# Idle matmuls ahead of the first loads, and attention loads moved from SyncE's queue to GpSimd's

## The chip, the cores and the metric

The kernel runs on one core of a Trainium2 chip. The metric is the device time of one execution in microseconds (us); the time of a kernel is the median of its runs. Engines are named as in the profile: PE is TensorE's matmul, PEld its weight load, DVE VectorE, ACT ScalarE, POOL GpSimd, SP SyncE, which issues most transfers.

## What is computed

Causal attention with a local mask (heads 0 to 3: the last 32 positions) and a strided mask (heads 4 to 7: same position modulo 32), then two MLPs one behind the other, all in float32. Weights arrive as 64-bit floats and are converted on the chip.

```
q, k, v: (4, 8, 576, 64)          # batch, heads, positions, head size
scores = q @ k.T / sqrt(64), masked with local (h < 4) or strided (h >= 4)
x  = softmax(scores) @ v          # transposed to (2304, 512)
h  = relu(x @ w_in)               # w_in (512, 2048)
x2 = (s * h*h + b) @ w_out        # w_out (2048, 512)
out = ((x2 @ w_a) * (x2 @ w_b)) @ w_o2
```

## The kernel before

The 2304 tokens are worked in six blocks of 384 columns. Block 0 holds positions 0 to 95 of the four batches, block 1 positions 96 to 191, and blocks 2 to 5 the rest of one batch each. The attention of block n+1 is worked in steps between the matmuls of block n's first MLP; block 0's attention has nothing to run beside and goes first.

**The first stage** (lines 758 to 782). `first_mask` builds the mask `fmask` on GpSimd: half 0 is local (L315, L319), half 1 strided (three selects, L324). `first_load` loads q, k and v of 96 positions for each batch on SyncE, 192 KB each; `stage_next` loads a pair of weight pieces (512 KB of `w_in` and 512 KB of `w_out`). Then `first` runs for each batch bb: PE transposes q and k (`fps`, L116), ACT copies them out (`fqkT`, L347), PE multiplies (`fss`, L113), the softmax follows (L210 on DVE adds the mask and takes the maximum, L216 on ACT is the exponential, L221 to L223 on DVE normalise), PE transposes the result (`fpp`), ACT copies it (`fpT`, L366), PE multiplies with v (`fpo`), and ACT and DVE split the product into a high and a low part of `x` (L131, L132). The tile `fqkT` of batch 0 lies in the one buffer with the tag "sk", which the second block's strided attention loads into afterwards.

**Weight conversion** (`to_float32`): L153 on ACT, L157, L160 and L163 on DVE, then the split L131 and L132. It is worked in the first stage too, in the gaps.

**Block 0's first MLP** then starts with `h_mm`: 12 matmuls of 128x384, the first that need all of `x`.

**Block 1's attention** (`local` with n == 1, and `strided_one`) is loaded ahead on SyncE: qn, kn, vn for the local heads and sk, sv for the strided ones.

A scheduler that models the engines' times (`schedule_with_timeline_sim=True`) sets the order of the instructions on each engine; on the chip each engine then takes them strictly in that order. A DMA issue waits at the head of its engine's queue until its buffer is free and until the DMA eight issues back in the same kind of queue has landed, since each kind has eight semaphores in turn (DMAHW0 to 7 for SyncE, DMASW0 to 7 for GpSimd in the order rows below).

Of the kernel before, what the change touches and what calls it, by code (L numbers as in the profile page):

```python
# [8 lines left out]
F32 = mybir.dt.float32  # L9
# [8 lines left out]
P = 128  # L18
# [8 lines left out]
def sparse_attention_two_mlps(  # L27
# [22 lines left out]
    nc = tc.nc  # L50
    B, H, S, D = q.shape
# [60 lines left out]
    def mm(*args, **kwargs):  # L112
        last_pe[:] = [nc.tensor.matmul(*args, **kwargs).ins]  # L113
# [118 lines left out]
    def local(spans, n, hp_, c0):  # L232


        (ba, ta), (bz, tz) = spans
        joint = ba == bz
        wk = QT if joint else P
        nk = (wk + P) // 2
# [5 lines left out]
        else:  # L244
            pieces = [(ba, ta, QT, 0, 0), (bz, tz, QT, QT // 2, P // 2)]
        for bb, t0, m, pq, pk in pieces:
            nc.sync.dma_start(
                out=qn[pq:pq + m // 2],
                in_=q[bb, hs, t0:t0 + m, :].rearrange("h (p j) d -> p h (j d)", j=2),
            )  # L250
            nc.sync.dma_start(
                out=kn[pk:pk + (m + STR) // 2],
                in_=k[bb, hs, t0 - STR:t0 + m, :].rearrange("h (p j) d -> p h (j d)", j=2),
            )
# [15 lines left out]
                    )  # L270
        yield
        for j, (bb, t0) in enumerate(spans):
            nc.sync.dma_start(
                out=vn[:, j], in_=v[bb, hs, t0 - STR:t0 + QT, :].rearrange("h t d -> t h d")
            )
        yield
# [33 lines left out]
    def first_mask():  # L310

        m = slot(wpa, [QT, 2, QT], "fmask")
        nc.gpsimd.memset(m[:, 0], 0.0)
        nc.gpsimd.memset(m[:, 1], NEG)
        nc.gpsimd.affine_select(  # L315
            out=m[:, 0], in_=m[:, 0], compare_op=ALU.is_ge, fill=NEG, base=0,
            pattern=[[-1, QT]], channel_multiplier=1,
        )
        nc.gpsimd.affine_select(  # L319
            out=m[:, 0], in_=m[:, 0], compare_op=ALU.is_gt, fill=NEG, base=STR,  # L320
            pattern=[[1, QT]], channel_multiplier=-1,
        )
        for i in range(IQ):
            nc.gpsimd.affine_select(  # L324
                out=m[:, 1], in_=m[:, 1], compare_op=ALU.not_equal, fill=0.0, base=-i * STR,
                pattern=[[-1, QT]], channel_multiplier=1,
            )
        return m

    def first_load(dst, src, bb):  # L330
        nc.sync.dma_start(out=dst, in_=src[bb, :, 0:QT, :].rearrange("h t d -> t h d"))
# [151 lines left out]
    def strided_one(pair, i):  # L483
# [6 lines left out]
        for j in range(2):  # L490
            bb = 2 * i + j
            for h in range(2):
                head = HL + 2 * pair + h
                nc.sync.dma_start(
                    out=sk[:QT, 3 * j:3 * j + 2, h], in_=k[bb, head, 0:TU].rearrange("(c p) d -> p c d", p=QT)
                )
                nc.sync.dma_start(out=sk[:QT, 3 * j + 2, h], in_=q[bb, head, QT:TU])
        yield
        kqT = tl([P, S], "skT")
        for j in range(2):  # L500
# [4 lines left out]
        yield  # L505
        for j in range(2):
            for h in range(2):
                nc.sync.dma_start(
                    out=sv[:QT, 2 * j:2 * j + 2, h],
                    in_=v[2 * i + j, HL + 2 * pair + h, 0:TU].rearrange("(c p) d -> p c d", p=QT),  # L510
                )
# [228 lines left out]
    def column_sums():  # L740
# [16 lines left out]
        nc.vector.tensor_copy(out=b_col, in_=pc)  # L757
        yield

    fmask = first_mask()  # L760
    qks, vs = [], []
    for bb in range(B):
# [4 lines left out]
    for bb in range(B):  # L767
        first_load(qks[bb][:, 0], q, bb)
        first_load(qks[bb][:, 1], k, bb)
        if bb % 2:  # L770
            first_load(vs[bb - 1], v, bb - 1)
            first_load(vs[bb], v, bb)
            stage_next()
    banks = ((ps_acc, "acc"), (ps_a, "a"), (ps_acc, "acc"), (ps_a, "a"))
    gens = [first(bb, qks[bb], vs[bb], fmask, *banks[bb]) for bb in range(B)]
    live, step = list(range(B)), 0
# [97 lines left out]
```

## Time and profile before

| | |
|---|---|
| median of 3 runs | 1040.44 us (1040.05 to 1041.5) |
| the profiled execution | 1042.37 us |
| its span | 1040.5 us |
| PE busy | 997.3 us (96%) |
| DVE busy | 470.0 us (45%) |
| ACT busy | 461.7 us (44%) |
| POOL busy | 72.6 us (7%) |

The span runs from the first to the last instruction of the profiled execution. A busy share is a mean over the whole span; the stages differ, so the first 150 us are read from windows of their own. The granted TensorE clock is 1.00 at the upper of two levels (2.4 GHz) and 0.50 at the lower (1.2 GHz).

### The profile page before, as it was taken

How to read it: one execution, taken by the hardware profiler on the slowest of the kernel's cores; microseconds unless marked ns; L12 is line 12 of the kernel's file. 1: busy time of each engine (PE TensorE's matmuls, PEld its weight loads, DVE VectorE, ACT ScalarE, POOL GpSimd, SP SyncE). 2: the span in 40 equal slices, each digit the busy share in tenths (PEclk: the TensorE clock that was granted, in tenths of full speed). 3: DMA queues.
4: the chain of work that ended last, by engine and by line, in shares of the span. 5: the costliest groups of instructions: out<-in, count | busy, mean ns of one | idle time of the engine just before them, and what ended most of it. 6: DMA issues, size and time to landing. Idle time of an engine off the chain costs nothing.

```text
span 1040.5 us, 15811 instructions
## 1 busy us (share of the span) xinstructions
PE 997.3 (96%) x5984; PEld 936.0 (90%) x5984; DVE 470.0 (45%) x1246; ACT 461.7 (44%) x1291; POOL 72.6 (7%) x110
## 2 busy tenths in 40 slices
PE   6878979999999899999999999999999999999998
PEld 5768979999899899889999989999999999999997
DVE  5689755766878677576522221211211211211111
ACT  6677846665675666567532231311311311211212
POOL 3000000001233132100000000000000000000000
PEclk9988989999999999999999999999999999999999
DMA  9556422456454554644567710200200100000000
GB/s 190 190 185 183 152 56 78 144 157 195 142 142 136 175 138 139 194 140 148 192 196 252 249 32 2 61 1 1 61 1 1 61 1 1 31 1 1 31 1 30
DMA packets 109819, 106.37 MB, mean 102 GB/s; under 512 B 59568, under 2 KB 94640, under 8 KB 109744
## 3 DMA queue, kind: packets, MB, share of 16 engines
q1 hardware_dynamic: 104560, 86.49, 28.9%
q0 software_dynamic: 5184, 18.88, 4.8%
q8 instruction: 47, 0.77, 0.3%
q14 instruction: 28, 0.23, 0.1%
HBM read 77.03 MB, written 28.31 MB: 101 GB/s over the span
## 4 chain that ended last, share of the span: by engine, by line
PE 85%; DVE 6%; ACT 5%; DMA 3%; issue 1%; SPq 0%; ACTq 0%; DVEq 0%
PE acc L113 30%; PE h L113 18%; PE pb L113 14%; PE pa L113 14%; PE pss L113 2%; PE po L113 2%; PE ppt L116 2%; DMA o<-o1s 1%; DMA xr<-o 1%; PE fss L113 1%; DVE raw L160 1%; DVE w L132 1%; DVE raw L163 1%; DVE raw L157 1%; ACT r L560 1%
## 5 line engine op out<-in xcount | busy, mean ns | idle before, releaser
L113 PE MATMUL h<-x,w 128*128 128x384 f32 x1152 | 229.2, 348 | 3.4 <-DVE w L132 1.3
L113 PE MATMUL acc<-gt,w 128*128 128x384 f32 x1152 | 223.0, 341 | 3.2 <-ACT o1s L586 3.2
L113 PEld LDWEIGHTS h<-x,w 128*128 128x128 f32 x1152 | 205.4, 194 | 7.9 <-DVE w L132 1.6
L113 PEld LDWEIGHTS acc<-gt,w 128*128 128x128 f32 x1152 | 199.4, 189 | 7.4 <-ACT o1s L586 3.8
L641 DVE TENSOR_TENSOR ab<-pb,ab 128x384 f32<-128x384 f32 x72 | 40.1, 557 | 306.7 <-ACT ab L640 306.7
L113 PE MATMUL pb<-x,w 128*128 128x384 f32 x864 | 165.0, 337 | 0.0
L113 PE MATMUL pa<-x,w 128*128 128x384 f32 x864 | 162.1, 335 | 1.5 <-ACT ab L640 1.5
L113 PE MATMUL acc<-w,abt 128*128 128x512 f32 x648 | 161.8, 393 | 0.0
L640 ACT ACTIVATE ab<-pa 128x384 f32<-128x384 f32 x72 | 35.4, 491 | 282.4 <-PE pa L113 282.3
L113 PEld LDWEIGHTS pb<-x,w 128*128 128x128 f32 x864 | 153.6, 188 | 6.4 <-DVE x L132 0.3
L113 PEld LDWEIGHTS pa<-x,w 128*128 128x128 f32 x864 | 150.8, 188 | 2.6 <-ACT ab L640 2.5
L113 PEld LDWEIGHTS acc<-w,abt 128*128 128x128 f32 x648 | 120.5, 188 | 21.9
L560 ACT ACTIVATE r<-h 128x384 f32<-128x384 f32 x96 | 46.8, 488 | 115.6 <-PE h L113 115.3
L567 DVE TENSOR_TENSOR r<-r 128x384 f32<-128x384 f32 x80 | 48.8, 610 | 91.1 <-ACT gt L566 90.5
L132 DVE TENSOR_TENSOR abt<-ab,abt 128x384 fp32r<-128x384 f32 x72 | 40.2, 558 | 46.8 <-ACT abt L131 46.8
L131 ACT ACTIVATE w<-raw 128x512 fp32r<-128x512 f32 x68 | 44.8, 670 | 25.7 <-DVE raw L163 21.6
L568 DVE TENSOR_TENSOR gt<-r,gt 128x384 fp32r<-128x384 f32 x80 | 54.1, 676 | 4.5
L132 DVE TENSOR_TENSOR w<-raw,w 128x512 fp32r<-128x512 f32 x68 | 45.9, 685 | 21.7 <-ACT w L131 20.8
L131 ACT ACTIVATE abt<-ab 128x384 fp32r<-128x384 f32 x72 | 37.7, 524 | 40.2 <-DVE ab L641 40.2
L604 POOL DMA_DIRECT2D w2d<-w x36 | 20.0, 556 | 431.6 <-DVE w L132 358.9
L163 DVE SCALAR_TENSOR_TENSOR raw<-raw 128x512 uint32<-128x512 uint32 x68 | 46.5, 686 | 0.7
L160 DVE SCALAR_TENSOR_TENSOR raw<-raw 128x512 uint32<-128x512 uint32 x68 | 45.9, 685 | 0.5
(109 smaller groups left out, 878.7 us busy)
## 6 DMA issues: line engine op xcount, KB each, us to landing
w2d<-w POOLq DMA_DIRECT2D x36, 512.0 KB, 5.2
w<-w2d SPq DMA_DIRECT2D x36, 512.0 KB
raw<-in_moe_w_out_dram SPq DMA_DIRECT2D x28, 512.0 KB
raw<-in_moe_w_in_dram SPq DMA_DIRECT2D x16, 512.0 KB
raw<-in_moe_w_a_dram SPq DMA_DIRECT2D x12, 512.0 KB
raw<-in_moe_w_b_dram SPq DMA_DIRECT2D x12, 512.0 KB
xr<-o SPq DMA_DIRECT2D x6, 768.0 KB
o<-o1s SPq DMA_DIRECT2D x20, 192.0 KB
```

The lines of the kernel that those rows point to most:

```text
L113: last_pe[:] = [nc.tensor.matmul(*args, **kwargs).ins]
L116: last_pe[:] = [nc.tensor.transpose(*args).ins]
L131: nc.scalar.activation(out=hi, in_=src, func=AF.Copy)
L132: return eng_lo.tensor_tensor(out=lo, in0=src, in1=hi.bitcast(F32), op=ALU.subtract)
L160: nc.vector.scalar_tensor_tensor(out=low, in0=high, scalar=3, in1=low, op0=ALU.logical_shift_left, op1=ALU.bitwise_or)
L163: nc.vector.scalar_tensor_tensor(out=high, in0=high, scalar=0x80000000, in1=low, op0=ALU.bitwise_and, op1=ALU.bitwise_or)
L560: relu = nc.scalar.activation(out=r, in_=ph, func=AF.Relu)
L567: nc.vector.tensor_tensor(out=r, in0=r, in1=r, op=ALU.mult)
L568: lo = nc.vector.tensor_tensor(out=gt[:, 1], in0=r, in1=gt[:, 0].bitcast(F32), op=ALU.subtract)
L604: stores.append(nc.gpsimd.dma_start(out=w2d[i - 1], in_=w.bitcast(F32)).ins)
L640: nc.scalar.activation(out=ab, in_=pa, func=AF.Copy)
L641: nc.vector.tensor_tensor(out=ab, in0=pb, in1=ab, op=ALU.mult)
```

## The change

Three edits. Ahead of the first stage PE gets 14 matmuls of the identity with itself into a PSUM tile that nobody reads. The loads of block 1's attention, in `local` and in `strided_one`, are issued by GpSimd in place of SyncE. The four v loads of the first stage go behind the first two pairs of weight pieces.

```diff
@@ local
         (ba, ta), (bz, tz) = spans
+
+        queue = nc.gpsimd if n == 1 else nc.sync
         joint = ba == bz
@@
         for bb, t0, m, pq, pk in pieces:
-            nc.sync.dma_start(
+            queue.dma_start(
                 out=qn[pq:pq + m // 2],
...
-            nc.sync.dma_start(
+            queue.dma_start(
                 out=kn[pk:pk + (m + STR) // 2],
...
         for j, (bb, t0) in enumerate(spans):
-            nc.sync.dma_start(
+            queue.dma_start(
                 out=vn[:, j], in_=v[bb, hs, t0 - STR:t0 + QT, :].rearrange("h t d -> t h d")
             )
@@ strided_one
-                nc.sync.dma_start(
+                nc.gpsimd.dma_start(
                     out=sk[:QT, 3 * j:3 * j + 2, h], in_=k[bb, head, 0:TU].rearrange("(c p) d -> p c d", p=QT)
                 )
-                nc.sync.dma_start(out=sk[:QT, 3 * j + 2, h], in_=q[bb, head, QT:TU])
+                nc.gpsimd.dma_start(out=sk[:QT, 3 * j + 2, h], in_=q[bb, head, QT:TU])
@@
-                nc.sync.dma_start(
+                nc.gpsimd.dma_start(
                     out=sv[:QT, 2 * j:2 * j + 2, h],
@@ the first stage
+    idle = ps_acc.tile([P, P], F32, tag="acc", name="idle")
+    for _ in range(14):
+        mm(idle, lhsT=ident, rhs=ident, start=True, stop=True)
+
     fmask = first_mask()
@@
         first_load(qks[bb][:, 0], q, bb)
         first_load(qks[bb][:, 1], k, bb)
         if bb % 2:
-            first_load(vs[bb - 1], v, bb - 1)
-            first_load(vs[bb], v, bb)
             stage_next()
+    for bb in range(B):
+        first_load(vs[bb], v, bb)
```

The lines below `local` move down by 2, those below the idle matmuls by 7. The scheduler makes a new order from the new program. Three places of it:

GpSimd's queue in the first stage, before (the selects of `fmask`, with those of the later masks `smask` and `omask` between them):

```order
L315 AFFINE_SELECT fmask_178<-fmask_178 96x96 [waits Pool_49]
L324 AFFINE_SELECT fmask_178<-fmask_178 96x96 [waits Pool_49]
L193 AFFINE_SELECT smask_148<-smask_148 84x126 [waits Pool_49]
L193 AFFINE_SELECT omask_149<-omask_149 96x192 [waits Pool_49]
L319 AFFINE_SELECT fmask_178<-fmask_178 96x96 [waits Pool_49]
```

and the same place of the change (sv and sk are block 1's strided loads; ten loads of qn, kn, vn and sv are issued by then):

```order
L326 AFFINE_SELECT fmask_193<-fmask_193 96x96 [waits Pool_49]
L510 DMA sv_614<-in_v_dram 96x2x64 [waits DMASW0_49]
L510 DMA sv_614<-in_v_dram 96x2x64 [waits DMASW1_49]
L496 DMA sk_613<-in_k_dram 96x2x64 [waits DMASW2_49,PE_49,Activation_49]
L321 AFFINE_SELECT fmask_193<-fmask_193 96x96 [waits Pool_49]
L499 DMA sk_613<-in_q_dram 96x64 [waits DMASW3_49]
L496 DMA sk_613<-in_k_dram 96x2x64 [waits DMASW4_49]
L499 DMA sk_613<-in_q_dram 96x64 [waits DMASW5_49]
L496 DMA sk_613<-in_k_dram 96x2x64 [waits DMASW6_49]
L326 AFFINE_SELECT fmask_193<-fmask_193 96x96 [waits Pool_49]
```

The last select of `fmask`'s local half (L321) now stands behind the first sk load, which waits for PE, and the last two of its strided half (L326) behind all eight sk loads.

DVE at the start, before (the first softmax, then the first weight piece):

```order
L210 ISA fpt_229,mx_240<-fss_230,fmask_178 96x96 [waits PE_49,Pool_49]
L210 ISA fpt_229,mx_250<-fss_235,fmask_178 96x96 [waits PE_49]
L221 TENSOR_SCALAR sm_241<-sm_241 96x4 [waits Activation_49]
L222 RECIPROCAL sm_241<-sm_241 96x4 [waits DVE_49]
L157 TENSOR_SCALAR raw_202<-raw_202 128x512 [waits DMAHW0_49]
```

and of the change, from the first softmax on (raw_223 is the second piece of w_in, raw_225 the second of w_out; the first two pieces are worked ahead of this):

```order
L210 ISA fpt_244,mx_265<-fss_250,fmask_193 96x96 [waits PE_49]
L157 TENSOR_SCALAR raw_223<-raw_223 128x512 [waits DMAHW4_49]
L160 SCALAR_TENSOR_TENSOR raw_223<-raw_223 128x512 [waits DVE_49,Activation_49]
L157 TENSOR_SCALAR raw_225<-raw_225 128x512 [waits DMAHW5_49]
L163 SCALAR_TENSOR_TENSOR raw_223<-raw_223 128x512 [waits DVE_49]
L160 SCALAR_TENSOR_TENSOR raw_225<-raw_225 128x512 [waits DVE_49,Activation_49]
L163 SCALAR_TENSOR_TENSOR raw_225<-raw_225 128x512 [waits DVE_49]
L210 ISA fpt_244,mx_255<-fss_245,fmask_193 96x96 [waits Pool_49]
```

Four of the 32 L210 (batch 0's local heads) now stand ahead of the second pair of weight pieces and 28 behind it, and the pair waits for its loads (DMAHW4 and DMAHW5).

SyncE's queue, before:

```order
L331 DMA fv<-in_v_dram 96x8x64 x2
L139 DMA raw<-in_moe_w_in_dram 128x4x256
L144 DMA raw<-in_moe_w_out_dram 128x1024
L247 DMA qn<-in_q_dram 48x2x128
L251 DMA kn<-in_k_dram 64x2x128
```

and of the change:

```order
L333 DMA fqk<-in_k_dram 96x8x64
L139 DMA raw<-in_moe_w_in_dram 128x4x256
L144 DMA raw<-in_moe_w_out_dram 128x1024
L333 DMA fv<-in_v_dram 96x8x64 x4
L406 DMA sq<-in_q_dram 128x3x64 x2
```

Before, twelve loads of 96x8x64 and four weight pieces stand up to the end of the second pair; in the change eight and four, with the v loads behind.

## Rows read from the trace of the kernel before

**Rows 1.** Windows: busy us (count) of PE, PEld, DVE, ACT, POOL; granted clock, DMA share, GB/s.
```profile
10.98:39.39 28.41, 25.18 (x166) 20.59 (x165) 23.82 (x109) 24.68 (x92) 0.08 (x1) 1.00 0.96 241
60.00:140.00 80.00, 67.07 (x448) 62.94 (x446) 70.81 (x185) 63.15 (x171) 0.00 (x0) 0.91 0.48 148
...
600.00:700.00 100.00, 99.08 (x520) 92.24 (x519) 21.51 (x40) 26.67 (x55) 0.00 (x0) 1.00 0.09 25
```

**Rows 2.** Timeline, first stage: start, duration, engine, line, what, idle before and releaser.
```profile
5.01 0.26 POOL L324 TENSOR_SCALAR_AFFINE_SELECT fmask<-fmask 96x96 f32<-96x96 f32 x1
...
10.69 0.26 DVE L210 CUSTOM_DVE_ANT_0 fpt<-fss,fmask 96x96 f32<-96x96 f32 x1 [9.34 <-PE fss L113]
...
14.50 0.43 DVE L157 TENSOR_SCALAR raw<-raw 128x512 uint32<-128x512 uint32 x1 [0.41 <-DMA raw<-in_moe_w_out_dram]
...
24.38 0.42 DVE L157 TENSOR_SCALAR raw<-raw 128x512 uint32<-128x512 uint32 x1
...
38.90 0.49 ACT L131 ACTIVATE x<-fpo 128x384 fp32r<-128x384 f32 x1 [0.48 <-PE fpo L113]
...
40.81 3.89 PE L113 MATMUL h<-x,w 128*128 128x384 f32 x11 [0.68 <-DVE x L132]
```

**Rows 3.** Groups of ACT by form, 10.9 to 39.4 us: count, busy us, mean ns, idle before.
```profile
L216 ACT ACTIVATE fpt<-fpt,mx 96x96 f32<-96x96 f32 x32 | 11.6, 364 | 3.8 <-DVE mx L210 3.8
...
L366 ACT ACTIVATE fpT<-fpp 96x384 f32<-96x384 f32 x8 | 3.8, 481 | 1.9 <-PE fpp L116 1.9
L153 ACT ACTIVATE raw<-raw 128x512 f32<-128x512 f32 x6 | 3.8, 671 | 0.0
...
L131 ACT ACTIVATE w<-raw 128x512 fp32r<-128x512 f32 x4 | 2.5, 663 | 0.0
L131 ACT ACTIVATE x<-fpo 128x384 fp32r<-128x384 f32 x4 | 1.9, 476 | 0.5 <-PE fpo L113 0.5
```

**Rows 4.** One form, transposes of 96x96, by source line: ns min/median/max, first and last start.
```profile
L116 PE MATMUL fpp<-ident,fpt x32: 364/367/396, 17.7 to 35.7; 96*96 96x96 f32 x32
...
L116 PE MATMUL ppt<-ident,spo x8: 246/246/287, 115.8 to 116.4; 96*96 96x96 f32 x8
```

**Rows 5.** PE's timeline: h_mm at either clock, and the form nearest to the idle matmuls.
```profile
45.28 4.21 PE L113 MATMUL h<-x,w 128*128 128x384 f32 x12 [0.58 <-ACT r L560]
...
50.44 2.33 PE L113 MATMUL h<-x,w 128*128 128x384 f32 x12
...
82.74 1.04 PE L113 MATMUL pss<-kT,qz 128*96 128x128 f32 x8
83.70 0.89 PE L113 MATMUL pss<-skT 64*96 64x192 f32 x8
```

**Rows 6.** Waits of PE, 40 to 150 us, and of SyncE's queue, 0 to 150 us.
```profile
PE ppt L116 <- DVE lpt L223: 7.6, 2, 5.4
PE ppt L116 <- DVE spo L223: 2.7, 1, 2.7
...
SPq L273 <- PE po L113: 29.2, 4, 12.0
```

**Rows 7.** DMA issues by GpSimd, source L604: count, ns min/median/max.
```profile
L604 POOL DMA_DIRECT2D w2d<-w x36: 531/535/691, 179.7 to 506.7; - x36
```

**Rows 8.** Windows of the first loads, columns as in rows 1.
```profile
5.00:13.00 8.00, 5.79 (x32) 4.55 (x32) 1.57 (x17) 3.00 (x12) 5.30 (x20) 1.00 1.26 247
13.00:20.00 7.00, 5.96 (x39) 5.79 (x40) 6.37 (x30) 6.08 (x26) 0.00 (x0) 1.00 1.33 194
...
20.00:22.00 2.00, 2.00 (x16) 1.78 (x15) 1.47 (x5) 1.96 (x8) 0.00 (x0) 1.00 1.09 347
```

**Rows 9.** The page's costliest groups: a conversion step of DVE.
```profile
L163 DVE SCALAR_TENSOR_TENSOR raw<-raw 128x512 uint32<-128x512 uint32 x68 | 46.5, 686 | 0.7
```

**Rows 10.** Windows in which the clock fell, columns as in rows 1.
```profile
66.50:67.00 0.50, 0.04 (x1) 0.00 (x0) 0.50 (x2) 0.42 (x2) 0.00 (x0) 1.00 1.08 408
67.00:68.00 1.00, 0.00 (x0) 0.00 (x0) 1.00 (x3) 0.64 (x2) 0.00 (x0) 0.51 0.86 338
```

## The prediction

> **What bounds the kernel now.** I read the table of windows first, to find the stages, then the timeline of the first 60 us, then the waits. From about 150 us on PE is the bound (99.1 of 100 us busy in 600 to 700, [rows 1]): nothing that this change touches runs there, so whatever it does to the start is carried unchanged to the end. The start is another matter. Until 40.8 us the first stage works block 0's attention, and the reader sees in [rows 2] that the first softmax step (L210) starts at 10.69 and the first matmul that needs all of x at 40.81. Between, ACT is busy for 24.7 of 28.4 us, PE for 25.2 and DVE for 23.8 [rows 1]: three engines that hand work round, ACT the nearest to being full once its own waits are counted [rows 3]. From 60 to 140 us DVE paces (70.8 of 80 us busy, PE 67.1).
>
> The clock column says 1.00 for the first stage, but that only means that no change had been recorded yet. The durations say otherwise: a 96x96 transpose takes 367 ns between 17.7 and 35.7 us and 246 at 116 [rows 4], and twelve h matmuls take 4.21 us at 45 and 2.33 at 50 [rows 5]. So PE works at the lower level, 1.2 GHz, until about 49.5 us, though it is busy most of the time. That is what the idle matmuls could change. SyncE's queue stood for 29.2 us behind one line of loads that waited for PE [rows 6], and that is what GpSimd's queue could change; but neither PE's waits [rows 6] nor DVE's name a load from 40 to 150 us.
>
> **Idle matmuls: 0.** 14 float32 matmuls of 128x128 are 28 records of the form of pss, of which eight go by in 83.70 - 82.74 = 0.96 us at the upper level, 0.12 each [rows 5]; at the lower twice that. So 3.4 to 6.7 us from about 1.5 us on, when the identity is built, and 8.2 us at the latest. They hide behind the first loads: the work behind them cannot be finished before k of batch 1 lands (below). Without that cover they would cost about 2 us, since the first transposes ran from 6.1 us.
>
> **Loads on GpSimd, later sets: 0.** Three more sets of 18 loads go to GpSimd, which has no other work from 25 to 180 us. 36 issues of its own kind took 531 to 691 ns [rows 7]. No engine waited for these loads before, and no weight behind them was late, so freeing SyncE gains nothing either.
>
> **Loads on GpSimd, first set: this is the cost.** Two things are queued behind them on GpSimd. The local half of fmask now stands behind the first sk load, and the strided half behind all eight. The sk loads write the buffer of batch 0's fqkT, so the first of them waits for batch 0's fss on PE. Before, fmask was done at 5.27 us [rows 2] and fss in time for 10.69. Now fss stands behind k of batch 1, and up to ten GpSimd loads (0.56 MB, 2.3 us at the 247 GB/s of [rows 8]) share the engines with it: my estimate is 13 to 15 us. Eight issues at 0.535 us [rows 7] and five selects of about 0.27 [rows 2] give 15 + 4.3 + 1.4 = 20.7 us for the whole mask, 15 later than before.
>
> But that isn't the last wait. The scheduler filled the gap with work: DVE now takes four L210, then the conversion of the second pair of weight pieces, and only then the other 28. The pair has to land. Before, its w_out piece stood behind twelve loads of 196.6 KB and three pieces of 524.3 KB: 4.46 MB with itself. Now it is eight such loads, four pieces and the 18 GpSimd loads (0.85 MB): 4.52 MB. The transfer engines were saturated throughout [rows 8], so I take bytes as time and only 0.06 MB, 0.2 us, as the difference. When did it land before? The first w_out piece released DVE at 14.50 [rows 2]; 2.23 MB follow, 1.07 at 194 GB/s until 20 us and 1.16 at 347 [rows 8], 23.3 us; and the L157 at 24.38 found it there. So 23.5 us now. Behind it stand one L157 of 0.42 and three steps of 0.69 [rows 2, 9]: 26.0, and the first exponential of the 28 at 26.3.
>
> From there ACT has, up to the last x: 28 exponentials of 364 ns (10.2 us), 3.8 for fpT, 1.9 for x, 2.5 for four w, one L153 of 0.67: 19.1 us [rows 3]. What it saved itself by waiting is six copies fqkT, five L153 and four exponentials. Its waits for PE (1.9 + 0.5, [rows 3]) I keep, since PE is no faster; its waits for mx I drop, since DVE has the next batch ready. 26.3 + 19.1 + 2.4 = 47.8 in place of 38.90 + 0.49 = 39.4 [rows 2]: 8.4 us later. The last x of DVE was 0.8 us late behind conversions before, and that goes. So the stage ends between 7.6 and 8.4 us later; I take 8.0. With no waits at all in ACT it would be 5.5, and with all 3.7 us of idle time of before [rows 1] 9.3.
>
> **v loads last: 0.** They land after the second pair, 0.79 MB or about 4 us later, by 28 us; the first fpo comes after 30 us.
>
> **Sum.** h_mm starts 8.0 us later, PE is still at the lower level there, and nothing behind it changes kind. The profiled execution took 1042.37 us (span 1040.5) and would take 1050.4; the median of the runs stands 1.93 below the profiled one, so 1048.4 us.
>
> **Two rules weighed.** The row says that a DMA issue on GpSimd costs 0.535 us, 0.691 at most, beside a busy DVE [rows 7]. The Trainium skill ("SBUF — State Buffer", section "SBUF: two separate sides") speaks against this change: such an issue cannot write its descriptors while DVE runs an operation that takes the port they share, and a transfer of 620 ns became one of 3100. By that, eight issues would put the mask at 41 us and the kernel at about 1063; by the row, which is this kernel's own, the mask is no bound, and I go by the row. The other: no row before 180 us shows the two queues loading at once. The Trainium skill ("DMA: Bandwidth & Descriptors", section "Rules for kernel authors") says that spreading DMAs over issuing engines gives no bandwidth, as all run on the same 16 engines. By it the sum stands; were it otherwise, the rival of the early pair below is what follows.
>
> **The rivals.**
> *The clock stays up.* If the idle matmuls raise the clock and the first stage's small work holds it until h_mm, the two h of 12 take 2.33 each in place of 4.21 (3.8 us) and ACT waits half as long for PE (1.2): 1048.4 - 5.0 = 1043.4. For it: the idle matmuls are as dense as the h that raised it at 49.5. Against: the first stage's transposes and small products left it low although PE was busy 25.2 of 28.4 us [rows 1, 4], and it fell at 67 us once PE had little to do [rows 10]; now PE idles while it waits for the mask.
> *The pair lands early.* If GpSimd's loads don't slow SyncE's, the 0.85 MB come off: 2.5 us at 347 GB/s to 4.4 at 194, and the exponentials start at about 22, just behind the mask: 1044.4. Against: a DMA share above 1 in [rows 8]. With the clock up as well, 1039.4: the change would then do nothing that can be measured.
> *GpSimd's issues are dear.* Above (26.0 - 20.7) / 8 + 0.535 = 1.2 us each the mask is later than the pair; at 2.0 it is done at 32.4 and the kernel takes 6 us more, 1054.5. These loads have more and shorter rows than those of [rows 7].
> *DVE gives it back, and more: faster.* In 60 to 140 us PE is idle for 12.9 us [rows 1], 10.3 of them before ppt, for DVE [rows 6]. If the new order there lets DVE run on without its 9.2 us of idle time and ppt come in time, all of 12.9 comes back: 1035.5. It decides for faster only where over 10 us come back. Against: the order of DVE hardly differs there, and it is short of time, not of data.
>
> **How the numbers follow.** Chances: my forecast 0.56 (about 1045 to 1051), clock up 0.10, early pair 0.09, both 0.09, dear issues 0.08, DVE gives back 0.08. A measurement of this kernel tells about 0.2%, 2.1 us, from no change. Slower: 0.56 + 0.10 + 0.09 + 0.08, less 0.04 for the ends of the clock and early-pair cases that fall below 1042.5: 0.79. Same: 0.09 + 0.04 = 0.13. Faster: 0.08. The range from 1039 to 1053 leaves out the fastest case and the dear issues, 0.16.
>
> **What would show it.** Right: four L210 near 15 us, the other 28 from 26, DVE's wait before them put down to the weight load; the first dense h at 48 to 49; eleven h in 3.9 us; from there a shift of about 8 us at every later step. Wrong: 28 L210 that wait for POOL (dear issues); a pair worked before 21 us (early pair); fpp at 246 ns or twelve h in 2.3 us (clock); a shift at 150 us much smaller than at 48 (DVE gave it back).

## The result, and the profile after

The change takes 1054.58 us (median of 4 runs, 1053.81 to 1057.64), the kernel before 1040.24 on the same chip: a ratio of 1.0146, 95% interval 1.0125 to 1.0167, so 14.3 us slower. The forecast was 8.2 us slower, with a range that ended at 1053. The direction was right, the size was not. In four of the experiments below (e5, e9, e13, e14) one or two executions took 1200 us or more, and the ratios leave these out.

The profiled execution took 1054.53 us, its span 1052.7. Windows of it, to be read against [rows 1] (start:end, length, then busy time and instructions of PE, PEld, DVE, ACT, POOL, then granted clock, DMA share, GB/s):

```profile
26.80:49.60 22.80, 18.86 (x129) 14.94 (x129) 15.69 (x88) 18.31 (x74) 0.00 (x1) 0.50 0.84 280
70.00:150.00 80.00, 66.37 (x431) 61.89 (x430) 68.75 (x179) 61.07 (x164) 27.15 (x42) 0.87 0.33 99
600.00:700.00 100.00, 99.42 (x525) 92.91 (x524) 21.51 (x40) 28.98 (x59) 0.00 (x0) 1.00 0.17 51
```

From 600 to 700 us PE is the bound as before, as forecast: 99.4 of 100 us. The first stage is where the prediction put the cost, but it lost more than forecast, and 70 to 150 us lost too: PE is busy 66.4 of 80 us at a mean clock of 0.87.

GpSimd's first loads and the mask (timeline of POOL: start, length, instruction, and in brackets what it waited for):

```profile
13.36 0.65 POOL L496 DMA_DIRECT2D sk<-in_k_dram  x1 [2.66 <-ACT fqkT L349]
14.02 0.28 POOL L321 TENSOR_SCALAR_AFFINE_SELECT fmask<-fmask 96x96 f32<-96x96 f32 x1
14.23 0.55 POOL L499 DMA_DIRECT2D sk<-in_q_dram  x1
...
18.29 0.28 POOL L326 TENSOR_SCALAR_AFFINE_SELECT fmask<-fmask 96x96 f32<-96x96 f32 x1
19.05 0.26 POOL L326 TENSOR_SCALAR_AFFINE_SELECT fmask<-fmask 96x96 f32<-96x96 f32 x1
```

DVE behind it, after its first four softmax steps:

```profile
17.61 0.25 DVE L210 CUSTOM_DVE_ANT_0 fpt<-fss,fmask 96x96 f32<-96x96 f32 x1
21.56 0.43 DVE L157 TENSOR_SCALAR raw<-raw 128x512 uint32<-128x512 uint32 x1 [3.69 <-DMA raw<-in_moe_w_in_dram]
...
24.08 0.47 DVE L157 TENSOR_SCALAR raw<-raw 128x512 uint32<-128x512 uint32 x1 [0.68 <-DMA raw<-in_moe_w_out_dram]
...
26.57 0.25 DVE L210 CUSTOM_DVE_ANT_0 fpt<-fss,fmask 96x96 f32<-96x96 f32 x1
```

So far it is the forecast's story with its numbers: the first sk load waits until 13.36 (the profile puts that down to ACT's copy into fqkT), the mask is whole at 19.3, and DVE stands in front of the second weight pair until 24.1, with the mask long done, and takes up the other 28 softmax steps at 26.57. ACT from there to its last x (the first exponential of the 28, the two longest waits, the last x):

```profile
26.86 0.38 ACT L216 ACTIVATE fpt<-fpt,mx 96x96 f32<-96x96 f32 x1 [2.09 <-DVE mx L210]
29.52 0.38 ACT L216 ACTIVATE fpt<-fpt,mx 96x96 f32<-96x96 f32 x1 [1.11 <-DVE fpt L223]
...
39.35 0.38 ACT L216 ACTIVATE fpt<-fpt,mx 96x96 f32<-96x96 f32 x1 [1.39 <-DVE mx L210]
...
49.05 0.47 ACT L131 ACTIVATE x<-fpo 128x384 fp32r<-128x384 f32 x1
```

In 26.8 to 49.6 ACT was busy 18.31 of 22.80 us, so it waited 4.5: 1.3 for PE and 3.2 for DVE. Of the two long waits for DVE, the 1.11 at 29.52 has DVE busy with its own softmax steps; at 39.35 (1.39) DVE had itself waited for PE's fss, which its line shows, followed by PE's:

```profile
39.00 0.25 DVE L210 CUSTOM_DVE_ANT_0 fpt<-fss,fmask 96x96 f32<-96x96 f32 x1 [1.08 <-PE fss L113]
```

```profile
29.57 0.85 PE L116 MATMUL fpp<-ident,fpt 96*96 96x96 f32 x4 [9.03 <-DVE fpt L223]
30.68 0.88 PE L116 MATMUL fpp<-ident,fpt 96*96 96x96 f32 x4 [0.27 <-DVE fpt L223]
31.49 2.35 PE L113 MATMUL fss<-fqkT 64*96 64x96 f32 x16
...
37.37 1.59 PE L113 MATMUL fss<-fqkT 64*96 64x96 f32 x8
...
39.69 1.59 PE L113 MATMUL fss<-fqkT 64*96 64x96 f32 x8
...
49.57 0.69 PE L113 MATMUL h<-x,w 128*128 128x384 f32 x1 [0.90 <-ACT x L131]
51.22 3.89 PE L113 MATMUL h<-x,w 128*128 128x384 f32 x11 [0.96 <-DVE x L132]
55.69 2.36 PE L113 MATMUL h<-x,w 128*128 128x384 f32 x12 [0.58 <-ACT r L562]
```

PE had nothing for 9.03 us and then a backlog at the lower level (fss of 8 in 1.59 us): fss of the later batches stand in PE's queue behind fpp and fpo of the earlier ones, so the softmax of batch 3 could not start before 39.0. The first h that needs all of x starts at 51.22 in place of 40.81 [rows 2], 10.4 us later, not 8.0.

### The profile page after: what moved, and what is told of

Read it like the earlier page. It is cut to its first block, busy times and chain, and to the rows that moved or that the text cites. A ratio compares the mean times of both kernels' runs of the same rounds, so it can differ in the third digit from the quotient of the medians.

```text
span 1052.7 us, 15887 instructions
## 1 busy us (share of the span) xinstructions
PE 1000.9 (95%) x6012; PEld 939.1 (89%) x6012; DVE 473.7 (45%) x1246; ACT 462.5 (44%) x1291; POOL 119.8 (11%) x182
## 4 chain that ended last, share of the span: by engine, by line
PE 83%; DVE 7%; ACT 5%; DMA 2%; SPq 1%; issue 1%; POOL 0%; ACTq 0%; DVEq 0%; POOLq 0%
PE acc L113 30%; PE h L113 17%; PE pb L113 14%; PE pa L113 14%; PE pss L113 2%; PE po L113 2%; PE ppt L116 1%; DMA o<-o1s 1%; SPq L333 1%; DVE raw L160 1%; DVE raw L157 1%; DVE w L132 1%; DVE raw L163 1%; DMA raw<-in_moe_w_out_dram 1%; ACT raw L153 1%
## 5 line engine op out<-in xcount | busy, mean ns | idle before, releaser
L163 DVE SCALAR_TENSOR_TENSOR raw<-raw 128x512 uint32<-128x512 uint32 x68 | 47.5, 704 | 0.8
L153 ACT ACTIVATE raw<-raw 128x512 f32<-128x512 f32 x68 | 44.3, 672 | 6.0 <-DMA raw<-in_moe_w_out_dram 3.4
```

The lines of the kernel that those rows point to most:

```text
L153: nc.scalar.activation(out=high.bitcast(F32), in_=high.bitcast(F32), func=AF.Copy, scale=HIGH_SCALE)
L163: nc.vector.scalar_tensor_tensor(out=high, in0=high, scalar=0x80000000, in1=low, op0=ALU.bitwise_and, op1=ALU.bitwise_or)
```

## The experiments

Times are medians; the ratio is to runs of the kernel before on the same chip. A trace is one execution: those of e8, e12 and e14 are the fastest of their runs (1041.29, 1039.40 and 1040.60 us), so they need not show all that the medians show. "DVE rows moved" counts the rows of DVE behind the first stage that stand in another order than in the kernel before. The last two columns are starts and distances of the same instructions in each trace: the first h of 11 of block 0, and the time from the acc that starts at 61.56 in the kernel before to the one at 147.59 there. (h is a product with a piece of w_in, acc one with a piece of w_out, 12 matmuls each.)

```
                                    us   ratio [95%]            DVE rows  h of 11   acc to
                                                                moved     at        acc
before                         1040.24                              0     40.81     86.0
the change                     1054.58   1.0146 [1.0125,1.0167]    47     51.22     90.8
e1  14 idle matmuls alone      1045.88   1.0053 [1.0034,1.0072]    16     40.42     88.8
e2  GpSimd's loads alone       1058.25   1.0173 [1.0157,1.0190]    73     54.86     89.3
e3  v loads last alone         1042.95   1.0025 [1.0013,1.0037]    18     40.76     88.8
e4  mask first                 1044.33   1.0041 [1.0028,1.0054]   136     42.19     87.1
e5  16 idle matmuls alone      1042.88   1.0023 [1.0013,1.0032]     0     see e13
e6  mask first, 20 idle        1045.46   1.0049 [1.0033,1.0065]     0     43.83     86.6
e7  pair behind, DVE           1055.68   1.0141 [1.0123,1.0159]    63     51.32     89.3
e8  first set on SyncE         1043.92   1.0035 [1.0022,1.0048]    15     40.47     88.2
e9  pair behind, DVE and ACT   1049.83   1.0093 [1.0079,1.0108]     4     47.71     88.1
e10 the change without idle    1055.82   1.0151 [1.0137,1.0165]    47     52.12     90.2
e11 7 idle alone               1039.51   0.9992 [0.9983,1.0002]     0     40.60     85.9
e12 8 idle alone               1041.51   1.0014 [1.0005,1.0023]    47     39.28     89.6
e13 16 idle, once more         1042.93   1.0022 [1.0011,1.0032]     0     40.87     85.8
e14 mask first, pair behind    1043.22   1.0027 [1.0017,1.0038]     2     43.28     86.0
e15 10 narrow idle alone       1040.44   1.0003 [0.9993,1.0013]     0     40.22     86.2
e16 before, second trace       1039.41   (one execution)            0     40.78     86.3
e17 change, second trace       1056.71   (one execution)           47     51.31     90.5
```

### One part of the change alone (e1 to e3)

e1 is the kernel before with the change's lines for `idle` and nothing else. e2 is the change without them and with the v loads back in their place:

```
-    idle = ps_acc.tile([P, P], F32, tag="acc", name="idle")
-    for _ in range(14):
-        mm(idle, lhsT=ident, rhs=ident, start=True, stop=True)
...
+            first_load(vs[bb - 1], v, bb - 1)
+            first_load(vs[bb], v, bb)
             stage_next()
-    for bb in range(B):
-        first_load(vs[bb], v, bb)
```

e3 is the kernel before with only that last hunk reversed (v loads last).

> The kernel before with the 14 idle matmuls alone; all loads on SyncE, v loads where they were. Theory (the whole loss comes from the first GpSimd loads standing ahead of the mask): nothing that a measurement can tell, 1038.5 to 1042.5; 28 idle records from about 1.5 us, the clock up for some microseconds after 5, low again well before the first h. Rival (order on PE): the scheduler now puts all 16 transposes of batches 0 and 1 ahead of batch 0's fss, which then wait for k of batch 1; the first softmax step slips from 10.7 to about 12.5 and the kernel is 2 to 4 us slower, 1042 to 1044. Rival (clock): the h of 12 take 2.3 us from the start and the kernel gains 2 to 4 us, 1036 to 1038.

> The kernel before with block 1's attention loads on GpSimd alone; no idle matmuls, v loads where they were. Theory: it alone gives nearly all of the change's loss, 1050 to 1056; the last select of the mask at about 18 to 20 us, the last x of ACT at 47 to 50. Rival (the three parts share the loss, the v loads by bringing the second weight pair ahead, the idle matmuls by PE's order): 1043 to 1049.

> The kernel before with the v loads of block 0 behind all q, k and weight loads of the first stage, alone. Theory: no change that can be told, 1038.5 to 1042.5, since the first product with v comes after 30 us and k of batches 2 and 3 comes only some 2 us sooner, where nothing waits for it. Rival: DVE's or ACT's order changes so that the second pair is worked earlier in the first stage and the exponentials later, 1043 to 1046.

GpSimd's loads alone cost 18.1 us, more than the whole change and more than e2's theory had (1050 to 1056): with the v loads ahead of it the second pair lands later still (DVE's wait for its w_in piece ends at 26.85, not 21.56, and h of 11 starts 3.6 us later). So v last, which I priced at nothing, seems to save some 2 us beside GpSimd's loads (e2 against e10: 2.7 us at h of 11; the two intervals of the ratio overlap a little). But e1 and e3 were slower too, by 5.7 and 2.8 us, though in both h of 11 starts no later. None of my expectations named the place: e3 loses it between the two acc, 88.8 us in place of 86.0. e1 loses as much there and another 2.7 us near 438 us, to which I come with e13.

### The first set and the mask (e4, e8, e6)

e4 holds every load of block 1 behind the mask's last two selects on GpSimd (masked holds these two instructions; the same around qn, kn, vn and sv):

```
+                with after(masked):
                     nc.gpsimd.dma_start(
                         out=sk[:QT, 3 * j:3 * j + 2, h], in_=k[bb, head, 0:TU].rearrange("(c p) d -> p c d", p=QT)
                     )
```

e6 is e4 with `range(20)` for the idle matmuls. e8 puts the first of the four sets back on SyncE (the second hunk is in `strided_one`, whose loads then go to `queue`):

```
-        queue = nc.gpsimd if n == 1 else nc.sync
+        queue = nc.gpsimd if n == 1 and (spans[0][0], hp_) != (0, 0) else nc.sync
...
+        queue = nc.gpsimd if (pair, i) != (0, 0) else nc.sync
```

> The changed kernel, with GpSimd's loads of block 1 held behind the last two selects of the mask on GpSimd itself; everything else as changed. Theory (the order on GpSimd is the cause): mask done by 7 us, first softmax step at 11 to 13, the last x of ACT at 40 to 42, the kernel at 1039 to 1044. Rival (the loads' bytes share the transfer engines with the weight pieces, whichever engine issues first): the second pair still lands at 24 and holds DVE, 1050 or more. Rival (GpSimd's issues and transfers slow DVE's stage behind, 60 to 160 us): x in time at 40 to 42, but the shift grows again by 3 to 4 us behind it, 1044 to 1047.

> The changed kernel with the first of the four sets of block 1's loads back on SyncE; the other three stay on GpSimd, idle matmuls and v loads last as in the change. Theory (only the first set costs, by the mask): first h of 11 at 40 to 42; behind it the same reordering as with the idle matmuls alone (15 steps of DVE), so 1042 to 1047. Rival (the later sets cost too, by issues that slow DVE or transfers that come late): a shift that grows by more than 3 us between 60 and 160 us, 1048 or more.

> The changed kernel with the mask ahead of GpSimd's loads as before, and 20 idle matmuls in place of 14, which gives DVE behind the first stage the order of the kernel before (136 steps stood elsewhere with 14). Theory (two causes only, the late mask and the other order behind): 1039.5 to 1042.5, the first h of 11 at 41 to 42.5 and the shift shrinking to 1 us or less behind it. Rival (loads on GpSimd cost something of their own from 60 us on): 1043.5 to 1046 as with 14.

Mask first takes 10.2 of the 14.3 us back, the first set on SyncE 10.7: the first set is the cost. How much of it is the late mask and how much the weight pair, e4 does not tell apart: with an early mask the planner puts 16 softmax steps ahead of the second pair, not four, so both waits shrink at once. 1044.33 lies just above e4's theory and inside its second rival's range, but not for the rival's reason (a shift that grows from 60 to 160 us): against the first trace of before the shift is 1.4 us at h of 11 and 0.8 at the second acc. The later three sets on GpSimd cost nothing that e1 has not got without them. A rest stays with mask first: h of 11 starts at 42.19 (e4) and 43.83 (e6), against 40.47 in e8. PE's last transposes of q and k show it, first in e8, then in e4:

```profile
15.30 0.87 PE L116 MATMUL fps<-ident,fqk 96*128 96x96 f32 x4 [0.48 <-DMA fqk<-in_q_dram]
16.46 0.87 PE L116 MATMUL fps<-ident,fqk 96*128 96x96 f32 x4 [0.28 <-DVE sm L221]
```

```profile
17.59 0.88 PE L117 MATMUL fps<-ident,fqk 96*128 96x96 f32 x4 [0.34 <-DMA fqk<-in_q_dram]
19.44 0.87 PE L117 MATMUL fps<-ident,fqk 96*128 96x96 f32 x4 [0.98 <-DMA fqk<-in_k_dram]
```

With GpSimd's first set in flight PE waits for the last k of block 0 until 19.44; in e8 that k was there before 16.46. That this delays the first stage is read from the traces, not tried by itself. The rate was no higher for it (first e8, then e4; the last number is GB/s):

```profile
5.00:13.00 8.00, 6.66 (x60) 6.20 (x60) 2.23 (x12) 3.14 (x7) 5.37 (x20) 1.00 1.23 254
13.00:20.00 7.00, 5.47 (x34) 4.05 (x34) 6.25 (x38) 6.46 (x30) 0.00 (x0) 0.61 1.23 256
```

```profile
5.00:13.00 8.00, 5.93 (x55) 5.29 (x56) 1.79 (x10) 2.31 (x5) 6.80 (x14) 1.00 1.20 247
13.00:20.00 7.00, 4.20 (x28) 3.13 (x26) 5.92 (x36) 4.77 (x20) 5.64 (x11) 0.53 1.23 219
```

So the second queue moves other bytes sooner and the first stage's own bytes later. e6 missed its expectation of 1039.5 to 1042.5: its order behind is right and its acc to acc of 86.6 us too, but its first stage ends 3 us late, and it shares e1's longer wait near 438 us (1.54 us).

### The second weight pair (e7, e9, e14)

e7 holds DVE's work on the second pair behind the last softmax step, e9 that of DVE and ACT behind the last softmax step and the last exponential (red and exp hold these instructions):

```
-    for _ in range(EARLY):
-        next_weights()
+    for i in range(EARLY):
+        with after(red + exp if i == 1 else []):
+            next_weights()
```

e14 is e9 with e4's mask and 7 idle matmuls.

> The changed kernel with DVE's work on the second pair of weight pieces held behind the last softmax step of the first stage; the mask is as late as in the change. Theory (DVE's queue stood on the second pair from 17.8 to 26.6 us, the mask being done at 19.3): the 28 softmax steps start at 19 to 20 us, the last x of ACT at 42 to 45, the kernel at 1046 to 1050. Rival (PE's chain of transposes and small products at the lower clock sets the end of the stage, however early the softmax starts): the last x at 47 or later, 1052 or more.

> The changed kernel with the work on the second pair of weight pieces held behind the softmax of the first stage on DVE and on ACT (with DVE alone, ACT's two L153 of the pair still stood in front of the fifth exponential and waited for the load). The mask is as late as in the change; DVE and ACT have behind the first stage the order of the kernel before but for 4 steps. Theory (two queues stood on the second pair; 19 us, the mask, is what is left): first 28 exponentials from 19 to 21, the last x at 42 to 45, the first h of 11 at 44 to 46.5, the kernel at 1043 to 1048. Rival (PE's chain at the lower clock sets the stage's end): the last x at 47 or later, 1050 or more.

> The changed kernel (GpSimd's loads, v last) with both causes taken away: the mask ahead of GpSimd's loads, the second pair behind the softmax on DVE and ACT; 7 idle matmuls, with which DVE and ACT have behind the first stage the order of the kernel before but for 2 steps each. Theory (the two are all of the cost): first h of 11 at 39.5 to 41.5, the kernel at 1038 to 1041.5. Rival (a third cost is left, loads of two queues that share the transfer engines with the weight pieces, or PE's order): first h of 11 at 42.5 or later, 1042.5 to 1045.

e7 gave nothing, and its trace says why. DVE was free, but ACT's two L153 of the pair (L154 there) stood between the first four exponentials and the fifth, and waited for the same load:

```profile
24.30 0.66 ACT L154 ACTIVATE raw<-raw 128x512 f32<-128x512 f32 x1 [1.08 <-DMA raw<-in_moe_w_out_dram]
24.86 0.37 ACT L217 ACTIVATE fpt<-fpt,mx 96x96 f32<-96x96 f32 x1
```

That fifth exponential is still 2.0 us sooner than in the change (26.86), and the stage ends no sooner: the pair's conversions now stand at its end, where four w of ACT (2.34 us from 45.13) go ahead of its last fpT. So e7 met its rival's range (1052 or more), but not as the rival had it, by PE alone.

With both engines freed (e9) the 28 steps start 6.1 us sooner, at 20.43, h of 11 starts 3.5 us sooner and the kernel gains 4.8, less than the theory had it (1043 to 1048) and just under the rival's bound of 1050. What holds it now is the mask, and behind it PE's backlog:

```profile
20.43 0.25 DVE L211 CUSTOM_DVE_ANT_0 fpt<-fss,fmask 96x96 f32<-96x96 f32 x1 [2.48 <-POOL fmask L327]
...
34.79 0.25 DVE L211 CUSTOM_DVE_ANT_0 fpt<-fss,fmask 96x96 f32<-96x96 f32 x1 [1.08 <-PE fss L114]
37.12 0.25 DVE L211 CUSTOM_DVE_ANT_0 fpt<-fss,fmask 96x96 f32<-96x96 f32 x1 [1.53 <-PE fss L114]
```

So mask and pair are two waits, one behind the other, that end some 6 us apart, and taking the later one away gives at most the distance to the earlier. Both gone (e14) leaves 3.0 us (1.0027 in the ratio); its trace has h of 11 2.5 us late, with PE waiting for q and k again (until 17.67), but is only 1.2 us longer than e16's. e14's theory (1038 to 1041.5) missed; the time and the 43.28 of h of 11 are its rival's, a third cost that is left.

### The order behind the first stage (e11, e12, e15, e5, e13, e10)

The edit is the number in `range(...)` of the idle matmuls alone, on the kernel before: 7, 8, 16. e15 has 10 with `idle[:, :32]` and `ident[:, :32]`. e10 is the change without the idle lines.

> The kernel before with 7 idle matmuls and every other instruction on PE, DVE and ACT in the order of the kernel before. Theory (idle matmuls cost nothing themselves): 1039 to 1041.5. Rival (they cost 2 to 3 us by themselves, by the clock): 1042 to 1044.5, and the trace shows where: a low stretch that is longer than in the kernel before, at the same instructions.

> The kernel before with 8 idle matmuls, one more than in the run beside it. With 8 the scheduler gives DVE and ACT behind the first stage the very order of the changed kernel (47 steps of DVE and 20 of ACT stand elsewhere than before). Theory (that order costs 2 to 4 us, whatever brought it about): 1042 to 1045, with the growth between 85 and 105 us. Rival (the order behind is worth nothing, and the growth in the other runs is the clock's chance): the same as with 7 to within 1 us.

> The kernel before with 10 idle matmuls of 32 columns each. The first stage stands in another order (88 steps of PE, DVE and ACT), DVE behind it as before, ACT but for 2 steps. Theory (the order behind decides): within 1.5 us of the kernel before, 1038.7 to 1041.7, the shift at 60 us unchanged at 150. Rival (every new order of the first stage costs 2 us or more): 1042 to 1044.

> The kernel before with 16 idle matmuls (14 in the change), alone. With 14 the scheduler puts 16 steps of DVE and 14 of ACT in another order behind the first stage, between 85 and 104 us; with 16 both engines have there the order of the kernel before to the last row. Theory (the idle matmuls cost nothing themselves, their 5.7 us in the run with 14 come from that order and from the low clock behind it): 1038.5 to 1042, first h of 11 at 40 to 41, no growth of the shift behind 85 us. Rival (the matmuls themselves cost it, by a clock that falls more often later): 1044 to 1047 as with 14.

> The kernel with 16 idle matmuls once more, for its trace. Theory (the first stage is ordered differently and ends later): the first h of 11 at 42 to 43.5 instead of 40.8, the shift constant from there to 160 us. Rival (the clock): the first h at 40 to 41 and the shift growing where a low stretch is longer.

> The changed kernel without the idle matmuls; loads and v last as in the change, and DVE and ACT have behind the first stage the very order of the change. Theory (the idle matmuls are worth nothing in either direction): 1053 to 1056.5, as the change. Rival (they cost the 3 to 5 us that every version with them has over the kernel before): 1048 to 1052. Rival (they brought the clock up sooner, in the second h of 12 at 55.7): the second h of 12 takes 4.2 us and the kernel 1055.5 to 1058.5.

e11 and e12 differ by one idle matmul, and e12 has DVE's and ACT's order of the change behind the first stage. PE from 63 us to the h at 102.6 (lpt, spo and pT are tiles of the next block's attention), first with 7:

```profile
65.84 0.52 PE L116 MATMUL ppt<-ident,lpt 96*128 96x96 f32 x4 [2.20 <-DVE lpt L223]
69.06 1.49 PE L116 MATMUL ppt<-ident,spo 96*96 96x96 f32 x8 [2.69 <-DVE spo L223]
...
93.20 0.55 PE L113 MATMUL po<-pT,vn 128*64 128x96 f32 x8 [2.08 <-ACT pT L293]
...
98.57 3.40 PE L113 MATMUL acc<-gt,w 128*128 128x384 f32 x12
...
102.64 2.35 PE L113 MATMUL h<-x,w 128*128 128x384 f32 x12
```

then with 8:

```profile
63.24 0.52 PE L116 MATMUL ppt<-ident,lpt 96*128 96x96 f32 x4 [2.66 <-ACT gt L131]
67.72 1.48 PE L116 MATMUL ppt<-ident,spo 96*96 96x96 f32 x8 [3.96 <-DVE spo L223]
...
92.11 0.91 PE L113 MATMUL po<-pT,vn 128*64 128x96 f32 x8 [2.65 <-ACT pT L293]
...
97.78 4.21 PE L113 MATMUL acc<-gt,w 128*128 128x384 f32 x12
...
102.74 2.35 PE L113 MATMUL h<-x,w 128*128 128x384 f32 x12
```

With 8, PE comes to the first ppt 2.6 us sooner: h of 11 starts 1.3 us sooner, and one h behind it no longer waits for DVE's w, as it does with 7 and in the kernel before, whose line this is:

```profile
59.70 2.02 PE L113 MATMUL h<-x,w 128*128 128x384 f32 x10 [1.27 <-DVE w L132]
```

All of it is lost by 102.7. PE waits 3.96 in place of 2.69 us for spo, which is no more than its earlier coming; then 2.65 in place of 2.08 for pT; and then it stays longer at the lower level, so that the acc of 12 takes 4.21 us in place of 3.40. The table's last column has the same in the other traces: the seven whose DVE rows stand as before, or but for 2, need 85.8 to 86.6 us from acc to acc, all others 87.1 to 90.8, and the four with the change's order 89.6 to 90.8. The number of rows is no measure of it (e4's 136 rows go with 87.1 us, e9's 4 rows with 88.1). And the column overstates the cost: the first of its two acc comes 1.6 us sooner in the change's order and the next h gives that back. From h of 11 to the second acc e12 takes 1.9 us more than e11 (108.6 against 106.7), the change in its second trace 2.9 more than the kernel before in its first (109.7 against 106.8). So this order, DVE's 47 rows and ACT's 20 together, costs 2 to 3 us. The medians of e12 and e11 are 2.0 us apart, between the ranges of e12's theory and of its rival.

Seven idle matmuls cost nothing (e11: 0.9992, the interval holds 1), and taking the 14 out of the change gains nothing (e10 against it: 1.2 us slower, intervals that overlap; its second h of 12 takes 4.21 us, as e10's last rival had it, but so it does in e17, with the 14). e15 has a new order in the first stage, the old one behind, and no loss. What idle matmuls do is shift the planner's times, and with them its order. e5 and e13 don't fit: the order behind is the old one, h of 11 at 40.87, and still 2.7 us. e13's trace loses it later, where acc waits at 438 us for o1s, ACT's copy of an earlier acc that is stored as o, 2.74 us against 0.43 in e16, and the next h of 12 runs at the lower level (3.80 against 2.37). ACT had waited for an earlier store of o to land, 4.87 us against 2.58. First e16, then e13:

```profile
435.66 0.58 ACT L586 ACTIVATE o1s<-acc,sb 128x384 f32<-128x384 f32 x1 [2.58 <-DMA o<-o1s]
436.29 0.80 PE L113 MATMUL acc<-gt,w 128*128 128x384 f32 x3 [0.43 <-ACT o1s L586]
...
438.20 2.37 PE L113 MATMUL h<-x,w 128*128 128x384 f32 x12 [0.24 <-ACT r L560]
```

```profile
437.99 0.58 ACT L586 ACTIVATE o1s<-acc,sb 128x384 f32<-128x384 f32 x1 [4.87 <-DMA o<-o1s]
438.62 0.79 PE L113 MATMUL acc<-gt,w 128*128 128x384 f32 x3 [2.74 <-ACT o1s L586]
...
440.53 3.80 PE L113 MATMUL h<-x,w 128*128 128x384 f32 x12 [0.24 <-ACT r L560]
```

The change has that wait too (2.22 at 449.73). It goes with the number of idle matmuls: PE waits 1.5 to 2.7 us there in all nine traces with 14 or more, and 0.4 to 0.7 in all nine with 10 or fewer (e5's trace, of 1388 us, left out). So 14 or more go with a loss of their own (e13: 2.7 us, with the old order behind). A packet of 16 KB on an instruction queue (q8, 47 of them in an execution) goes the same way: in the nine it starts within 2 us of the first of these stores' issue, in the others 2.9 us or more behind it. From 431.5 to 435.5 us e13 has this line among its DMA queues, and e16 none for q8:

```profile
q8 instruction: 1, 0.02, 2.1%
```

That the idle matmuls move a load of PE's instructions onto the stores and hold them up fits these rows, and is not shown: no run moved the packet alone.

### The same two kernels once more (e16, e17)

> The kernel before, unchanged, for a second trace. Theory (when the clock rises and how long it stays low behind a gap is chance from run to run): a span of 1036 to 1040 us, shorter than the 1040.5 of the first trace, and the whole difference at a few places, the second h of 12 (4.2 us in the first trace) at 2.4 or a low stretch that is missing. Rival (it belongs to the program): the same spans of h, ppt and acc to within 0.3 us at every place, and the two spans within 1 us.

> The changed kernel, unchanged, for a second trace. Theory (chance): the order of events up to the last x of ACT within 0.5 us of the first trace (49.5), the second h of 12 at 2.4 or 4.2, and a span of 1051 to 1056. Rival (it belongs to the program): the second h of 12 again at 2.4, the same low stretches, span within 1 us of 1052.7.

The second h of 12 differs from execution to execution of one program, as the theory had it; with two traces each, chance is the plain reading. It is, in e16 and in e17:

```profile
45.24 2.39 PE L113 MATMUL h<-x,w 128*128 128x384 f32 x12 [0.58 <-ACT r L560]
```

```profile
55.78 4.21 PE L113 MATMUL h<-x,w 128*128 128x384 f32 x12 [0.58 <-ACT r L562]
```

The kernel before took 4.21 there in its first trace [rows 5] and 2.39 in its second, the change 2.36 and then 4.21. So the first two traces flatter the change by some 1.9 us. The first trace of before and e17, both with 4.21, are the pair to compare: 1040.5 and 1054.9, 14.4 us, which is the difference of the medians.

## Why the prediction was wrong, step by step

In that pair the 14.4 us are: 10.5 at the first h of 11; 2.9 more up to the second acc (4.5 between the two acc, less the 1.6 by which the first of them comes sooner, since the h that waited 1.27 us for DVE's w at 59.70 no longer does); 1.0 behind, which is 2.1 us regained near 350 us, where a shorter wait for o1s leaves the next h of 12 at the upper level (2.35 us in place of 3.22), and 3.5 lost again up to 480, most of it at the wait that stands at 438 us in e16. The forecast had 8.0 and then nothing.

- **Idle matmuls at nothing: right for the first stage, not behind it.** 28 records from 1.54 to 6.3 us, hidden. They did raise the clock: the first four fps took 0.49 us at 6.17, where such four take 0.9 at the lower level. But it was down again from 13.4 us on (fss of 16 in 2.34). That they move the planner's order was not in my list at all, nor was the wait near 438 us that every trace with 14 or more has; the two together are about all of e1's 5.7 us. In the change, taking them out gained nothing (e10), since the 2.1 us near 350 are not regained there either.
- **Later sets on GpSimd at nothing: right** (e8 against e1).
- **First set: right in kind.** Mask at 19.3 (forecast 20.7), pair at 24.08 (23.5), first of the 28 softmax steps at 26.57 (26.0), its exponential at 26.86 (26.3). That the pair and not the mask is the last wait is shown by e9.
- **First failed step: "its waits for mx I drop, since DVE has the next batch ready".** From 26.8 to 49.6 ACT was busy 18.3 us (forecast 19.1) and waited 4.5 (2.4). The waits for PE that I kept at 2.4 were 1.3; the waits for DVE that I dropped were 3.2. DVE did not have the next batch ready: 1.8 of the 3.2 came behind its own waits for PE's fss of batch 3, which stood in PE's queue behind fpp and fpo, at the lower level, and 1.1 while DVE was still at its own steps of the batch before. 8.4 + 0.6 + 2.1 - 0.8 = 10.3 us for the last x, measured 10.1 (49.52 against 39.39). The end of the stage, 10.4 us later, lies outside the bound of 9.3, which took before's idle time as the most there could be (the bound without waits, 8.0 - 2.4, is 5.6, not 5.5). The 0.4 us that I let the gap from x to h shrink did not come either; it grew by 0.3.
- **v loads last at nothing: not shown right.** Alone 2.8 us slower by the order behind (e3); beside GpSimd's loads about 2 us faster (e2 against e10), where the second pair lands sooner.
- **Second failed step: "nothing behind it changes kind", the shift "carried unchanged to the end".** It grew by 2.9 us from h of 11 to the second acc and by 1.0 behind. Against a rival I had written that "the order of DVE hardly differs there"; the order with 47 rows of DVE elsewhere is worth 2 to 3 us (e12), partly as waits and partly as time at the lower level behind them. Behind 150 us, where I had PE as the only bound, waits for o1s near 350 and 438 us still moved the end by 2 to 3.5 us each.
- **The 1.93 us between the profiled run and the median** was what the kernel before showed; the change's own profiled execution stands at its median (1054.53 against 1054.58). The second h of 12, 1.8 us shorter in e16, is the likely reason: e16's span is 2.9 us shorter in all.

The rivals: the clock did not stay up (fpp of 4 takes 0.88 at 30.68); the pair did not land early; GpSimd's issues were not dear (0.54 to 0.65 each), and that this rival's 1054.5 us is the measured time is luck; DVE did not give time back, the stretch it paces got longer. The mechanism of the first stage was the forecast's, with its waits for DVE too small; the growth behind it was a term put at nothing.

Of the two rules: GpSimd's sk loads were issued in 0.54 to 0.65 us while DVE worked on the first weight pair from 14.8 to 17.1 us. The Trainium skill ("SBUF — State Buffer", section "SBUF: two separate sides") has a DMA issued by GpSimd take some 3.1 us in place of 0.62 beside a DVE copy that holds the port they share; no issue in these rows is prolonged so, and the row was the better guide. (That figure is a transfer's; I had set it against an issue's.) Whether these DVE operations take that port, no run here shows. The first windows of e4 and e8 moved 247 and 254 GB/s with and without GpSimd's loads. The Trainium skill ("DMA: Bandwidth & Descriptors", section "Rules for kernel authors") has it that more issuing engines give no more bandwidth, and these traces agree; what I did not draw from it is that the loads that are then waited for come later.

## What to carry to other kernels

Ahead of moving loads to another engine's queue, list what that engine still has to do for the first stage, and force it in front: with three selects of some 0.27 us put back ahead of the loads, and the order that the planner then made, 10 of the 14 us were gone. If an order is planned by a program, compare the rows of every paced stage behind the edit too, and price a different order there as a cost of some us, of unknown sign, not as nothing: try the same edit with a size that leaves the order alone (7 idle matmuls and 8). Follow the shift to the end of the trace as well: 14 idle matmuls at the start went with a longer wait at 438 us. And where a queue is late, count the backlog on the in-order engine that it feeds: waits that were zero for lack of lateness come back.

## What the runs showed of the hardware that was not expected

- The same program has its second h of 12 at 4.21 us in one execution and at 2.39 in the next (e16, e17 and the first traces): in the one PE is at the upper level ahead of it, in the other only at its end, and this alone is worth 1.8 us of an execution.
- The 28 idle records brought PE to the upper level while they ran, and the transposes and small products behind them did not keep it there, though they had PE busy 18.9 of 22.8 us later on (0.50 granted from 26.8 to 49.6).
- A longer wait of PE can be paid for twice: in e12 the wait for pT is 0.57 us longer than in e11, and the acc of 12 behind it takes another 0.81, at the lower level; in e13 the wait for o1s is 2.3 us longer than in e16, and the h of 12 behind it takes another 1.4.
- A 16 KB packet of instructions on q8 and the stores of o fall together in all nine traces with 14 or more idle matmuls, and the last o1s then waits 3.7 to 4.9 us for a store, in place of 2.6 to 2.8. That the one holds up the other is not shown.
